# Attention and a four-expert mixture on one core: three preparations moved in the start of the program, and nine products put behind the last products with v

## The chip, the cores and the metric

The kernel runs on 1 core of one Trainium2 chip. The metric is device time in microseconds of one execution, the median of 3 runs. The matrix engine is called PE, its weight loads PEld; DVE, ACT, POOL and SP are the vector, scalar, GpSimd and sync engines. SP does no arithmetic here: it issues most of the DMAs.

## The reference

```python
def _attn_ref(q, k, v, n_global, n_local):            # (4, 8, 768, 64)
    scores = scale * np.matmul(q, k.transpose(0, 1, 3, 2))
    keep = is_global | is_local                        # 8 first keys, or 96 keys back
    scores = np.where(keep, scores + bias, -1e9)       # bias falls with distance, by head
    a = softmax(scores)
    return np.matmul(a, v)
def _moe_ref(x, domain_probs, w1, w2):                 # x: 3072 x 512, 4 experts, 1024 hidden
    p = domain_probs / (domain_probs.sum(-1, keepdims=True) + 1e-09)
    for e in range(E):
        h = np.maximum(x @ w1[e], 0.0)
        out += p[:, e:e + 1] * (h @ w2[e])
```

x is the attention's output, heads side by side. `domain_probs` is 3072 x 4 float32.

## The kernel before

**The work.** The rows are 4 batches of 768. The attention of batch 0 (`first_attention`) comes first and alone. The experts' products of batch 0 come next; beside them runs the attention of batches 1 to 3 (`attention`), and then the experts' products of batches 1 to 3 (`turned_batch`). A unit is one expert and 256 of its 1024 hidden columns, so a batch has 16 units. `first(i)` is x·w1 of unit i, `second(i)` is h·w2. The order is first(0), first(1), second(0), first(2), second(1) and so on.

**Products.** Each float32 operand is split in two rounded parts, high and low, and a product is three matmuls on them. x·w1 goes by a seven-product scheme of block matrices: on the weights' side A11, A12, A22 and the sums S1 to S4, on x's side B11, B21, B22 and the sums T1 to T4. `product(i, a, x)` is one of the seven, six matmuls of 384 columns into a PSUM tile `pm`, of which there are four in turn. The x side stands in tiles xB... and xT... that `forms_of` and `last_forms` fill: the high part by ACT (CAST), the low part by POOL or DVE (TENSOR_TENSOR). `load_w1` loads 512 KB of w1 into `raw`, POOL makes the four sums, and high and low parts go to `w1s`. `load_w2` does the same into `w2s`. A tile `raw` exists once for w1 and once for w2, so a load waits until the unit before is split. What has been split is written back to DRAM (`kept`) for the later batches.

**ReLU.** `relu` lets ACT write the high part of h, and `work_late` lets DVE write the low part later. A pm is free for another product only when both have read it.

**first_attention.** Twelve steps d work on two tiles of 128 rows for two heads each, in the order of pairs 0, 2, 1, 3. A step issues `scores` (PE), `softmax` (DVE: add bias and take the maximum, ACT: exponential), `turn` (PE transposes, DVE copies to pT), `turn_qk` (PE transposes of q and k of two steps later, ACT copies), `weigh_two` (PE: products with v and with the reciprocals; ACT copies the latter to rT) and `finish` (DVE multiplies into x). `weigh_two` has one PSUM tile, so that of step d can start only when `finish` of d - 1 has read it.

**Beside it.** The loop under `Ordered.on = True` hangs other work on the steps: `chores` are generators (`load_w1`, `load_w2`) that go on by one `yield` per step. Their arguments count steps: `load_w1(i, wait, lead, hold)` waits before the load, between load and sums, and between sums and split; `load_w2(i, lead, highs, gap)` waits `lead` steps between load and split and `gap` more between the two halves of the split. `mixture()` loads `prob`, and after its `yield` divides each row by its sum on DVE. After d = 13 comes the loop over `events`, which runs `first` and `second`. There instructions of DVE, ACT, POOL and SP keep the order of the program for the first `ONSTEPS` = 7 steps; after that a scheduler may place them.

**In steps 9 to 13** the loop starts `mixture()` (d = 9), starts `load_w2(0, ...)` (d = 10), and at d = 12 issues A11·B11 of unit 0 and the first half of A12·B21 (nine matmuls), ends the mixture and makes the form B21. At d = 13 it issues S1·T1 of unit 0 and A11·B11 of unit 1, and `last_forms`. Each of these comes after that step's own instructions, so what stands at d = 12 comes ahead of `weigh_two` of the last step, which belongs to d = 13.

Of the kernel before, what the change touches and what calls it, by code (L numbers as in the profile page):

```python
# [25 lines left out]
def f32(ap):  # L26
    return ap.bitcast(F32)
# [159 lines left out]
def attn_moe_kernel(ctx: ExitStack, tc, q, k, v, n_global, n_local, domain_probs, w1, w2, out):  # L187
# [19 lines left out]
    ve, ac, po, sy, te = (Ordered(tc, e) for e in (nc.vector, nc.scalar, nc.gpsimd, nc.sync, nc.tensor))  # L207
# [69 lines left out]
    def mixture():  # L277

        sy.dma_start(prob, domain_probs.rearrange("(t p) e -> p t e", p=P))
        yield  # L280

        psumm = fast.tile([P, P, 1], F32, name="psumm")[:, :NT]
        ve.reduce_sum(psumm, prob, axis=AX.X)
        ve.tensor_scalar_add(psumm, psumm, 1e-9)
        ve.reciprocal(psumm, psumm)
        ve.tensor_mul(prob, prob, psumm.to_broadcast([P, NT, E]))
# [213 lines left out]
    def first_attention(A, bank):  # L500
# [9 lines left out]
        def both(src, pr):  # L510
            return [src[0, 2 * pr + j].rearrange("(t p) d -> p t d", p=P) for j in range(2)]

        def start(pr, ts):
            if pr not in nats:
                nats[pr] = {m: A.nat.tile([P, NQT, 2, D], F32, name=f"first_{m}") for m in ("q", "k")}
            for m, src in (("q", q), ("k", k)):
                for j, rows in enumerate(both(src, pr)):
                    sy.dma_start(nats[pr][m][:, ts, j, :], rows[:, ts])

        def start_v(pr):  # L520
            vt, vg = (A.natv.tile([P, 2, NQT, D], F32, name=f"first_{m}") for m in ("v", "vg"))
            load_v(vt, vg, 0, pr)
            nats[pr]["v"], nats[pr]["vg"] = vt, vg
# [45 lines left out]
        def softmax(new):  # L569
            t, i, pr = new["t"], new["i"], new["pr"]  # L570
            bcol = slice(2 * P, 3 * P) if t == 0 else slice(0, 2 * P)
            pcol = slice(P, 2 * P) if t == 0 else slice(0, 2 * P)
            nmax = A.small.tile([P, 2], F32, name="nmax")
            new["pb"] = A.pb.tile([P, 2, 2 * P], F32, name="pb")
            for j in range(2):
                e = new["pb"][:, j, pcol]
                ve.tensor_tensor_reduce(
                    e, new["ps"][j], bias["n"][:, 2 * pr + j, bcol], 1.0, 3.0e38, ALU.add, ALU.min, nmax[:, j : j + 1]
                )
                ac.activation(e, e, AF.Exp, bias=nmax[:, j : j + 1], scale=-1.0, accum_out=new["z"][:, i, j : j + 1])  # L580
# [24 lines left out]
        def finish(d):  # L605
            pr, ts = tiles_of(d)
            ve.tensor_mul(x[:, pr, ts[0] * P : (ts[1] + 1) * P], pxs[d][:, : 2 * P], rTs[d])
# [9 lines left out]
        turn_qk(0)  # L617
        scores(0)
        start_v(ORDER[0])
        start(ORDER[1], slice(0, NQT))  # L620
        turn_qk(1)
        softmax(steps[0])
# [6 lines left out]
        for d in range(1, last + 3):  # L629
            if d + 1 <= last:  # L630
                scores(d + 1)
            if last - 1 <= d <= last + 1:
                finish(d - 3)
            if d <= last:
                softmax(steps[2 * d])
                softmax(steps[2 * d + 1])
            if d <= 3:
                next(spread)
            if 3 <= d < last - 1:
                finish(d - 3)  # L640
            if 1 <= d <= last + 1:
                for n in range(2):
                    turn(bank, A, steps[2 * d - 2 + n], ve.tensor_copy)
                recip(d - 1)
            if d + 2 <= last:
                turn_qk(d + 2)
            if d >= 2:
                weigh_two(d - 2)
            if d > last:
                finish(d - 2)  # L650
            if d % 3 == 1 and d // 3 + 2 < NPAIR:
                start(ORDER[d // 3 + 2], slice(0, NQT))
            if d % 3 == 2 and d // 3 + 2 < NPAIR:
                start_v(ORDER[d // 3 + 2])
            yield
# [157 lines left out]
    def load_w2(i, lead=7, highs=(ac.copy, ac.copy), gap=0):  # L813

        if i >= len(units):
            return
        b, e, g = units[i]
        if b >= TURNED and (e, g // 2) != (E - 1, NPR // 2 - 1):
            return
        if b > 0:  # L820
            wts[(i, 2)] = fetch("w2s", (e, g, 2), [P, 2, 2, DM], lambda t: t)
            return
        raw = rp.tile([P, 2, DM], F32, name="raw2")
        sy.dma_start(raw, w2[e, g * 2 * P : (g + 1) * 2 * P, :].rearrange("(a p) m -> p a m", p=P))
        for _ in range(lead):
            yield 1
        dst = wp.tile([P, 2, 2, DM], F32R, name="w2s")
        wts[(i, 2)] = dst
        for f in range(2):
            highs[f](dst[:, 0, f], raw[:, f])  # L830
            po.tensor_tensor(dst[:, 1, f], raw[:, f], f32(dst[:, 0, f]), op=ALU.subtract)
            yield 1
            for _ in range(gap * (1 - f)):
                yield 1
        waiting[(i, 2)] = (e, g, 2), dst
# [420 lines left out]
    chores = []  # L1256
# [17 lines left out]
    with ExitStack() as start_stack:  # L1274
        A = Pools(
            start_stack, "start",
            dict(setup=1, kd=2, qd=2, nat=2, natv=3, pb=6, pT=4, rT=2, small=6, sums=2), {},
        )
        for d, _ in enumerate(first_attention(A, bank)):
            if d == 0:  # L1280
                chores.append(load_w1(0, 0, 1, 1, po.tensor_copy))
            if d == 6:
                chores.append(load_w1(1, 0, 1, 0, po.tensor_copy))
            if d == 10:
                chores.append(load_w2(0, 2, (po.tensor_copy, ac.copy), 2))
            if d == 9:
                mix = mixture()
                next(mix)
            if d == 5:
                forms_of(0, ("B11", "T1"), ac.copy, po, ve, A)  # L1290
            if d == 8:
                forms_of(0, ("B21", "B22", "T3"), ac.copy, po, ve, A)
            if d == 9:
                forms_of(0, ("T2", "T4"), ac.copy, po, ve, A)
            if d == 11:
                forms_of(1, ("B11", "T1"), ac.copy, po, ve, A)
            if d == 12:
                p1, vv = up1.tile([P, HALF], F32, name="p1"), up.tile([P, HALF], F32, name="vv")
                ac.copy(p1, product(0, "A11", "B11")[:, :HALF])
                begun[1] = product(0, "A12", "B21", (0,))  # L1300
                next(mix, None)
                forms_of(1, ("B21",), ac.copy, ve, ve, A)
            if d == 13:
                begun[0] = p1, vv
                begun[2] = up1.tile([P, HALF], F32, name="p1")
                pms = product(0, "S1", "T1"), product(1, "A11", "B11")

                def take():
                    ve.tensor_add(vv, pms[0][:, :HALF], p1)
                    ac.copy(begun[2], pms[1][:, :HALF])  # L1310

                last_forms(1, take, A)
            work_chores()
    hp = early.enter_context(tc.tile_pool(name="hp", bufs=2))
    op = early.enter_context(tc.tile_pool(name="op", bufs=1))
    A = Pools(early, "att", dict(natv=1, ks=1, qs=1, nat=1, pb=2, pT=6, xt=2, small=2), {})
# [19 lines left out]
    for b in range(TURNED):  # L1336
        events = [(first, b * per)]
        for i in range(b * per + 1, (b + 1) * per):
            events += [(first, i), (second, i - 1)]
        events.append((second, (b + 1) * per - 1))  # L1340
        for n, (fn, i) in enumerate(events):
            if n == len(events) - 2:
                if b == TURNED - 1:
                    for _ in att:
                        pass
                chores.append(blocks(b + 1))
            if b == 0 and n == 0:
                chores += [load_w1(2, 1, 4, 1), load_w2(1, 6)]
            else:
                chores.append(load_w1(i + 2, 4) if fn is first else load_w2(i + 2))  # L1350
            if b == TURNED - 1 and n == len(events) - 12:
                chores.append(spread_shares())
            for _ in fn(i):
                work_chores()
                done += 1
                if done == ONSTEPS:
                    next(att)
                    check_sizes()
                    Ordered.on = False
                while emitted < count and emitted * (span - ONSTEPS) < (done - ONSTEPS) * count:  # L1360
                    next(att, None)
                    emitted += 1
# [43 lines left out]
```

## Time and profile before

| | |
|---|---|
| median of 3 runs | 1152.97 us (1152.83 to 1153.66) |
| the profiled execution: its time | 1152.95 us |
| its span, first to last instruction | 1151.2 us |
| PE busy | 1133.3 us (98%) |
| DVE busy | 890.4 us (77%) |
| POOL busy | 617.9 us (54%) |
| ACT busy | 551.7 us (48%) |
| mean granted TensorE clock | 0.999 of 2.4 GHz |

Times in rows are from the span's start; 1.75 us of the execution lie outside the span. A busy PE is one with a matmul in its pipeline, which does not say that it runs at its best rate. An idle engine is worth something only where PE in the end waits for it: PE is the engine with the least idle time, 17.9 us of the span.

### The profile page before, as it was taken

Reading aid. Unit: us, or ns where it says so; the run is one execution under the profiler, and the core shown is the slowest. Engines: PE = TensorE matmul, PEld = TensorE weight load, DVE = VectorE, ACT = ScalarE, POOL = GpSimd, SP = SyncE. Lnnn points to the kernel's source line nnn. Section 1 sums busy time; section 2 is a strip of 40 time slices with the busy share of each in tenths; the row PEclk is TensorE's granted clock in tenths of the full one; section 3 lists DMA queues with packets and bytes.
Section 4 is the critical chain, followed back from the end, with each engine's and each line's share of the span. In section 5 each row is a group of like instructions: output and inputs, shape, how many; then the busy total and the mean of one; then the engine's idle time right before and its main releaser. Section 6 shows DMA issues by size and latency. Waiting matters only on the chain.

```text
span 1151.2 us, 19555 instructions
## 1 busy us (share of the span) xinstructions
PE 1133.3 (98%) x7209; PEld 1064.8 (92%) x7209; DVE 890.4 (77%) x1618; ACT 551.7 (48%) x1337; POOL 617.9 (54%) x548
## 2 busy tenths in 40 slices
PE   8999999999999999999999999999999999999998
PEld 6778888888888889999999999999999899999996
DVE  6976677666676679788888867888889678888884
ACT  6748888788888733422222424222224253222231
POOL 5756434534343155766666357666662377766620
PEclk9999999999999999999999999999999999999999
DMA  8568887667876676666666565666666556666632
GB/s 204 138 201 312 266 258 225 222 211 220 272 252 218 209 277 231 227 222 229 243 243 241 195 211 214 227 222 224 262 239 235 213 202 234 219 233 220 219 120 95
DMA packets 184679, 256.26 MB, mean 223 GB/s; under 512 B 109216, under 2 KB 158976, under 8 KB 173568
## 3 DMA queue, kind: packets, MB, share of 16 engines
q1 hardware_dynamic: 177520, 231.34, 59.4%
q0 software_dynamic: 6048, 22.02, 5.0%
q10 hardware_dynamic: 1008, 1.57, 0.4%
q8 instruction: 59, 0.97, 0.3%
q14 instruction: 44, 0.36, 0.1%
HBM read 199.28 MB, written 55.62 MB: 221 GB/s over the span
## 4 chain that ended last, share of the span: by engine, by line
PE 83%; DVE 9%; ACT 4%; DMA 2%; issue 1%; SPq 1%; POOL 1%; ACTq 0%; DVEq 0%
PE pm L42 49%; PE pq L42 24%; PE pt L42 6%; PE ps L42 5%; DVE sumT L42 2%; DVE form L42 2%; DVE hB L42 1%; ACT pb L42 1%; DVE hT L42 1%; DMA w1s<-kept 1%; DVE pm L42 1%; DVE x L42 1%; DVE sumB L42 1%; SPq L42 1%; ACT form L42 0%
## 5 line engine op out<-in xcount | busy, mean ns | idle before, releaser
L42 PE MATMUL pm<-xT,w1s 128*128 128x384 f32 x1536 | 305.9, 336 | 0.8 <-DVE h L42 0.5
L42 PEld LDWEIGHTS pm<-xT,w1s 128*128 128x128 f32 x1536 | 268.3, 188 | 2.8 <-DVE h L42 1.6
L42 PE MATMUL pm<-xB,w1s 128*128 128x384 f32 x1152 | 224.7, 336 | 1.9 <-DVE hB L42 0.9
L42 PEld LDWEIGHTS pm<-xB,w1s 128*128 128x128 f32 x1152 | 201.0, 188 | 5.7 <-DVE hB L42 3.4
L42 POOL TENSOR_TENSOR raw<-raw 128x512 f32<-128x512 f32 x84 | 119.0, 1416 | 152.8 <-DMA raw<-in_moe_w_dram 147.8
L42 PE MATMUL pq<-form,w2s 128*128 128x384 f32 x1008 | 188.7, 334 | 0.0
L42 PEld LDWEIGHTS pq<-form,w2s 128*128 128x128 f32 x1008 | 176.0, 188 | 0.0
L42 PE MATMUL pm<-w2s,h 128*128 128x512 f32 x576 | 140.3, 395 | 1.6 <-DVE h L42 1.6
L42 PE MATMUL pq<-form,w2f 128*128 128x384 f32 x756 | 141.2, 334 | 0.0
L42 PEld LDWEIGHTS pq<-form,w2f 128*128 128x128 f32 x756 | 132.0, 188 | 0.0
L42 ACT CAST form<-hB 128x768 fp32r<-128x768 f32 x105 | 85.4, 836 | 92.4 <-DVE hB L42 92.4
L42 PEld LDWEIGHTS pm<-w2s,h 128*128 128x128 f32 x576 | 106.3, 188 | 22.9 <-POOL sums L42 1.5
L42 POOL TENSOR_TENSOR w2s<-raw,w2s 128x512 fp32r<-128x512 f32 x53 | 74.0, 1401 | 90.2 <-ACT w2s L42 78.4
L42 POOL TENSOR_TENSOR form<-hB,form 128x768 fp32r<-128x768 f32 x42 | 85.9, 2046 | 33.7 <-ACT form L42 33.7
L42 DVE TENSOR_TENSOR form<-hB,form 128x768 fp32r<-128x768 f32 x63 | 89.7, 1451 | 17.1 <-ACT form L42 16.8
L42 ACT ACTIVATE pb<-pb,nmax 128x256 f32<-128x256 f32 (+1 forms) x192 | 92.7, 488 | 11.4 <-DVE nmax L42 11.3
L42 ACT COPY p<-pm 128x384 f32<-128x384 f32 x64 | 30.7, 479 | 117.6 <-PE pm L42 117.4
L42 DVE SCALAR_TENSOR_TENSOR acc<-pm,prob,acc 128x512 f32<-128x512 f32 x90 | 67.0, 748 | 24.0 <-PE pm L42 23.1
L42 POOL TENSOR_TENSOR w2f<-raw,w2f 128x512 fp32r<-128x512 f32 x63 | 81.7, 1297 | 5.0
L42 POOL TENSOR_TENSOR w1s<-raw,w1s 128x512 fp32r<-128x512 f32 (+1 forms) x32 | 32.5, 1023 | 93.7 <-ACT w1s L42 93.3
L42 DVE TENSOR_TENSOR sumT<-pq,sumT 128x768 f32<-128x768 f32 x72 | 68.4, 950 | 17.4 <-PE pq L42 17.3
L42 DVE SCALAR_TENSOR_TENSOR hB<-pm,share 128x384 f32<-128x384 f32 x132 | 72.3, 553 | 6.7 <-PE pm L42 2.8
(157 smaller groups left out, 1795.6 us busy)
## 6 DMA issues: line engine op xcount, KB each, us to landing
w1s<-kept SPq DMA_DIRECT2D x48, 1792.0 KB, 8.6
w2s<-kept SPq DMA_DIRECT2D x126, 256.0 KB, 5.2
kept<-w1s SPq DMA_DIRECT2D x16, 1792.0 KB, 8.3
raw<-in_moe_w_dram POOLq DMA_DIRECT2D x42, 512.0 KB, 8.0
raw<-in_moe_w_dram SPq DMA_DIRECT2D x32, 512.0 KB, 4.5
kept<-w2s SPq DMA_DIRECT2D x16, 1024.0 KB, 7.1
w2s<-kept SPq DMA_DIRECT2D x6, 1024.0 KB, 4.8
v<-in_v_dram SPq DMA_DIRECT2D x12, 384.0 KB, 4.8
```

The lines of the kernel that those rows point to most:

```text
L42: ins = fn(*args, **kwargs)
```

## The change

Four edits, all in the start of the program.

1. The load of `prob` goes from step 9 to the start of first_attention, behind the loads of v of the first pair and ahead of those of q and k of the second pair. The four DVE instructions that normalize it go from d = 12 to d = 1.
2. `load_w2(0, ...)` has no gap: the second half of the split of unit 0's w2 comes two steps sooner.
3. The nine matmuls of A11·B11 and A12·B21, and the ACT copy that reads them, go from d = 12 to d = 13: behind weigh_two of the last step. The form B21 stays at d = 12.
4. `load_w1(2, ...)` waits for no step before its load, so that all of unit 2's w1 moves up by one step.

```diff
@@ first_attention @@
         start_v(ORDER[0])
+        mix = mixture()
+        next(mix)
         start(ORDER[1], slice(0, NQT))
...
                 softmax(steps[2 * d + 1])
+            if d == 1:
+                next(mix, None)
             if d <= 3:
@@ the loop around it @@
             if d == 10:
-                chores.append(load_w2(0, 2, (po.tensor_copy, ac.copy), 2))
-            if d == 9:
-                mix = mixture()
-                next(mix)
+                chores.append(load_w2(0, 2, (po.tensor_copy, ac.copy), 0))
...
             if d == 12:
+                forms_of(1, ("B21",), ac.copy, ve, ve, A)
+            if d == 13:
                 p1, vv = up1.tile([P, HALF], F32, name="p1"), up.tile([P, HALF], F32, name="vv")
                 ac.copy(p1, product(0, "A11", "B11")[:, :HALF])
                 begun[1] = product(0, "A12", "B21", (0,))
-                next(mix, None)
-                forms_of(1, ("B21",), ac.copy, ve, ve, A)
-            if d == 13:
                 begun[0] = p1, vv
@@ the loop over events @@
             if b == 0 and n == 0:
-                chores += [load_w1(2, 1, 4, 1), load_w2(1, 6)]
+                chores += [load_w1(2, 0, 4, 1), load_w2(1, 6)]
```

On SP, in the first microseconds: first_q and first_k are loads for batch 0, raw_248 and raw_249 are unit 0's w1. Before:

```order
L42 DMA first_v<-in_v_dram 128x12x64
L42 DMA first_vg<-in_v_dram 96x12x64
L42 DMA first_vg<-in_v_dram 32x6x64 x2
L42 DMA first_q<-in_q_dram 128x6x64 x2
L42 DMA first_k<-in_k_dram 128x6x64 x2
L42 DMA raw_248<-in_moe_w_dram 128x4x256
```

Now:

```order
L42 DMA first_v<-in_v_dram 128x12x64
L42 DMA first_vg<-in_v_dram 96x12x64
L42 DMA first_vg<-in_v_dram 32x6x64 x2
L42 DMA prob<-in_moe_domain_probs_dram 128x24x4
L42 DMA first_q<-in_q_dram 128x6x64 x2
L42 DMA first_k<-in_k_dram 128x6x64 x2
L42 DMA raw_249<-in_moe_w_dram 128x4x256
```

The load of prob, 128 x 24 pieces of 4 numbers, stands ahead of q and k of the second pair.

On PE, at the end of batch 0's attention: ps<-pT,... are products with v, ps<-ident,zr the reciprocals, pm<-xB... and pm<-xT... products with w1.

```order
 L42 MATMUL ps<-pT,first_v 64x128 x2
 L42 MATMUL ps<-ident,zr 64x128 x4
-L42 MATMUL pm<-xB_577,w1s 128x384 x6
-L42 MATMUL pm<-xB_775,w1s 128x384 x3
 L42 MATMUL ps<-pT,first_vg 64x128 x2
 L42 MATMUL ps<-pT,first_v 64x128 x2
```

The nine products no longer stand between the last two groups of products with v; they follow the second.

On ACT, where first(0) begins: h<-pm is a ReLU, p a copy of a product; raw_913 and raw_918 are unit 0's w2, raw_1121 and raw_1125 unit 1's w2, raw_1132 and raw_1123 unit 2's w1. Before:

```order
L42 COPY p_1038<-pm 128x384
L42 ACTIVATE h<-pm 128x384
L42 CAST w2s<-raw_913 128x512
L42 ACTIVATE h<-pm 128x384 x2
L42 CAST w2s<-raw_1121 128x512
L42 ACTIVATE h<-pm 128x384
L42 CAST w1s<-raw_1132 128x512
L42 CAST w2s<-raw_1121 128x512
```

Now:

```order
L42 COPY p_1038<-pm 128x384
L42 CAST w2s<-raw_918 128x512
L42 ACTIVATE h<-pm 128x384
L42 CAST w1s<-sums 128x512
L42 CAST w2s<-raw_1125 128x512
L42 ACTIVATE h<-pm 128x384
L42 CAST w1s<-sums 128x512
L42 ACTIVATE h<-pm 128x384 x2
L42 CAST w1s<-raw_1123 128x512
```

The cast of unit 1's w2 stood behind the third of unit 0's four ReLUs; it now stands behind the first, with a cast of unit 2's sums ahead of it.

## Rows read from the trace of the kernel before

**Rows 1.** Busy time by stretch: us, then busy (count) by engine, clock, DMA share, GB/s.

```profile
core 0: us, PE busy (x) PEld busy (x) DVE busy (x) ACT busy (x) POOL busy (x), PEclk, DMA share, GB/s
12.00:17.00 5.00, 3.66 (x28) 2.51 (x29) 2.93 (x14) 4.03 (x17) 0.00 (x1) 1.00 1.04 259
17.00:47.00 30.00, 29.99 (x336) 24.55 (x335) 27.17 (x99) 25.54 (x100) 24.52 (x29) 1.00 0.88 219
...
61.50:78.00 16.50, 13.74 (x71) 11.84 (x71) 12.89 (x27) 8.25 (x17) 5.78 (x7) 1.00 0.70 222
78.00:450.00 372.00, 371.44 (x2658) 328.47 (x2659) 259.50 (x707) 277.92 (x818) 161.78 (x162) 1.00 0.74 244
```

**Rows 2.** Timeline of PE: start, duration, what, count, idle time before and its releaser.

```profile
14.76 0.41 PE L42 MATMUL ps<-ident,first_k 128*128 128x128 f32 x2 [0.41 <-DMA first_k<-in_k_dram]
```

**Rows 3.** Timeline of SP: DMA issues.

```profile
10.28 1.13 SPq L42 DMA_DIRECT2D first_k<-in_k_dram  x2
...
32.60 0.39 SPq L42 DMA_DIRECT2D raw<-in_moe_w_dram  x1
33.03 0.51 SPq L42 DMA_DIRECT2D prob<-in_moe_domain_probs_dram  x1
33.58 2.95 SPq L42 DMA_DIRECT2D raw<-in_moe_w_dram  x1
...
68.46 0.90 SPq L42 DMA_DIRECT2D raw<-in_moe_w_dram  x2
```

**Rows 4.** Tile view of first_k, issues at 10.3 and 10.9 us: from issue to landing.

```profile
DMA to landing us min/median/max: 3.1/3.4/3.8
```

**Rows 5.** Tile view of prob: from issue to landing.

```profile
DMA to landing us min/median/max: 4.8/4.8/4.8
```

**Rows 6.** Tile view of raw, the issue at 32.60 us: from issue to landing.

```profile
DMA to landing us min/median/max: 3.8/3.8/3.8
```

**Rows 7.** Timeline of DVE, 12 to 74 us, seven of its rows.

```profile
13.74 1.13 DVE L42 COPY pT<-pt 128x256 f32<-128x256 f32 x2 [1.53 <-PE pt L42]
...
57.85 0.42 DVE L42 TENSOR_TENSOR x<-ps,rT 128x256 f32<-128x256 f32 x1 [0.33 <-ACT rT L42]
...
59.62 0.26 DVE L42 TENSOR_TENSOR prob<-prob,psumm 128x96 f32<-128x96 f32 x1
...
61.09 0.42 DVE L42 TENSOR_TENSOR x<-ps,rT 128x256 f32<-128x256 f32 x1 [0.74 <-ACT rT L42]
...
67.07 0.55 DVE L42 TENSOR_TENSOR vv<-pm,vv 128x384 f32<-128x384 f32 x1
...
69.11 0.56 DVE L42 SCALAR_TENSOR_TENSOR h<-pm,h 128x384 fp32r<-128x384 f32 x1
...
73.78 0.56 DVE L42 SCALAR_TENSOR_TENSOR h<-pm,h 128x384 fp32r<-128x384 f32 x1 [2.06 <-ACT h L42]
```

**Rows 8.** Timeline of PE, 55 to 87 us, seven of its rows.

```profile
55.81 0.44 PE L42 MATMUL ps<-pT,first_vg 128*64 128x128 f32 x4 [0.35 <-DVE x L42]
...
57.27 1.85 PE L42 MATMUL pm<-xB,w1s 128*128 128x384 f32 x9
59.05 0.44 PE L42 MATMUL ps<-pT,first_vg 128*64 128x128 f32 x4
...
60.51 1.31 PE L42 MATMUL pm<-xT,w1s 128*128 128x384 f32 x6
...
64.62 2.36 PE L42 MATMUL pm<-xT,w1s 128*128 128x384 f32 x12 [0.19 <-ACT p L42]
67.21 3.84 PE L42 MATMUL pm<-xT,w1s 128*128 128x384 f32 x18 [0.23 <-DVE h L42]
...
78.00 8.46 PE L42 MATMUL pm<-w2s,h 128*128 128x512 f32 x36 [1.23 <-DVE h L42]
```

**Rows 9.** Timeline of ACT, 66 to 74 us, two of its rows.

```profile
66.46 0.61 ACT L42 CAST w2s<-raw 128x512 fp32r<-128x512 f32 x1
...
72.73 0.62 ACT L42 CAST w2s<-raw 128x512 fp32r<-128x512 f32 x1 [2.07 <-DMA raw<-in_moe_w_dram]
```

**Rows 10.** Timeline of POOL, one row.

```profile
67.15 1.29 POOL L42 TENSOR_TENSOR w2s<-raw,w2s 128x512 fp32r<-128x512 f32 x1 [7.93 <-ACT w2s L42]
```

## The prediction

> **What bounds the kernel now.** I read the busy times by stretch first. From 78 to 450 us PE is busy 371.44 of 372 us [rows 1]. Whatever moves its first matmul there, the product h·w2 of unit 0 at 78.00 [rows 8], moves the end by as much; what is prepared sooner for later units buys nothing, because PE waits for none of it. So the question is when PE reaches that matmul. Before it there are three places where it waits. Around 14 us it stands 0.41 us for the keys of the second pair [rows 2]; from 17 to 47 us it is busy 29.99 of 30 us, so a delay at 14 us is carried through [rows 1]. Around 50 to 58 us, at the end of batch 0's attention, a group of products with v waits for DVE to empty the one PSUM tile [rows 8]. From 61.5 to 78 us PE is idle 2.76 us [rows 1], mostly because a ReLU's low part on DVE comes late and a `pm` is not free. The DVE timeline gives that its cause: at 73.78 DVE has stood 2.06 us for ACT [rows 7], and ACT stood 2.07 us in a cast that waited for unit 1's w2 from DRAM [rows 9]. That load was issued at 68.46 [rows 3], when POOL's second half of unit 0's w2 (67.15, 1.29 us) let go of `raw` [rows 10, 3].
>
> **The change, part by part.** The time is made against the profiled execution, 1152.95 us (its span is 1151.2); the median of the runs shown is 0.02 us above it.
>
> *The load of prob, sooner.* It is placed ahead of q and k of the second pair, whose last load is issued at 10.9 and lands 3.8 us later, at 14.7 [rows 4]; PE starts on it at 14.76 [rows 2]. There is no slack, and nothing can come out of this but a delay. The lower end is the issue alone: prob at 33.03, the next at 33.58 [rows 3], 0.55 us. The middle is its transfer: it landed at 33.03 + 4.8 = 37.8, the load issued ahead of it at 32.60 + 3.8 = 36.4 [rows 3, 5, 6], so it held the DMA engines 1.4 us. The upper end is the issue after it, which took 2.95 us where the like one took 0.39 [rows 3]: SP stood 2.5 us behind prob. The DMA engines are full where the load now goes (share 1.04 from 12 to 17 us, [rows 1]), so I take most of the transfer: **+1.2 us**, ends 0.55 and 2.5. The loads of batch 0 behind it in SP's queue are late by as much, and so is PE that wants them. POOL's queue is passed by nothing.
>
> The Trainium skill (DMA: Bandwidth & Descriptors, section Bandwidth, its table of measured sizes) gives a floor of about 10.5 ns a packet for small transfers. The 3,072 pieces of prob would take 32 us by it one after another, which the landing after 4.8 us denies [rows 5]; shared by 16 engines they would take 2.0 us, an estimate from that page, and with it in place of 1.2 the sum would be 1155.45.
>
> *The mixture's four DVE instructions.* They now stand ahead of the first copies to pT, before which DVE is idle 1.53 us from 12.2 on [rows 7]. In the old place they took 59.88 - 58.27 = 1.6 us [rows 7]. Prob lands by 9.2 + 4.8 = 14.0 at the latest by the old figure, so DVE could be done at 15.6, 1.9 us late; 1.2 us of that is PE's own delay, and DVE has 2.8 us of idle time from 17 to 47 us to catch up [rows 1]. Cost 0, upper end +0.7. Taking them out at 58 us is worth nothing by itself: the next row that matters, the last piece of x at 61.09, waited 0.74 us for ACT and not for them [rows 7]. They would be in the way after the next edit.
>
> *The nine products behind the last products with v.* Before, these products of 1.78 us (57.27 to 59.05, [rows 8]) lay over the wait for DVE's read at 57.85 to 58.27 [rows 7]. Now PE stands until 58.3 and starts the last products with v there instead of at 59.05. From that start to the last piece of x it is 61.09 - 59.05 = 2.04 us, so x is there at 60.3: **-0.74 us** for DVE's chain of forms. PE, though, gets to S1·T1 at 58.3 + 1.46 + 1.78 = 61.55 and not at 60.51 [rows 8]: **+1.05 us** for PE. Which of the two decides? DVE's sum of vv and S2·T2 at 67.07 [rows 7] begins as the twelve products from 64.62 end, at 66.98 [rows 8]: PE decides. With the 0.19 us wait gone that sum starts at about 67.9, +0.8.
>
> *Unit 0's w2 sooner, and unit 1's.* The cast is now ahead of the first ReLU: it can start when the copy of A11·B11 of unit 1 is made: twelve matmuls behind 61.55, and the copy, about 64.4. POOL's half follows and ends at 66.4, unit 1's w2 is issued then, 2 us sooner, and as before lands 4.25 us later (68.46 to 72.73, [rows 3, 9]), at 70.7. That looks like 2 us gained on the wait at 72.73. But the order on ACT has changed: that cast now stands ahead of the second ReLU of unit 0, where it stood ahead of the fourth. The second ReLU's input is ready at 67.9 + 0.9 + 0.6 = 69.4; ACT gets to it after the cast's 0.6 us [rows 9], at 71.3. Its low part on DVE starts at 71.7 instead of 69.11 [rows 7]. Behind it in DVE's queue wait the remaining sums of unit 0, and on PE the product S1·T1 of unit 1, which needs that `pm`: 72.3. Five more products of six matmuls at 197 ns (2.36 us for 12, [rows 8]) take 5.9 us, and I leave 0.3 us for the next low part: PE is at h·w2 at 78.5, where it was at 78.00. Together with the edit before: **+0.5 us**. The lower end, should ACT not hold the ReLU: 75 matmuls from 61.55 on without a wait make 76.35, -1.65. The upper end, should DVE fall behind a second time by as much as the 0.7 that its chain already lags: +1.2.
>
> *Unit 2's w1 sooner.* Its load goes ahead of batch 1's v in SP's queue and lands before 60 us. POOL's sums follow the split of w2. PE first wants the result at 87 us and does not wait there today [rows 1]. Worth 0; its casts on ACT are part of the jam above.
>
> **Sum:** 1152.95 + 1.2 + 0.5 = 1154.65, against the median 1154.7.
>
> **The rivals.**
> *A, the preparations pay:* prob costs its issue alone, and the cast of unit 1's w2 finds its data, so that no ReLU is held. Then PE runs from S1·T1 to h·w2 unbroken: 1152.95 + 0.55 - 1.65 = 1151.85. For it: the load does go out 2 us sooner, and the wait that it removes is the longest on that path. Against it: the order on ACT, and 4.25 us from issue to landing. It decides for A if the load lands before 69.4, which needs an issue at 65.1.
> *B, SP is held behind prob:* if SP stands 2.5 us there as it did at 33.58, the keys land near 17.1 and the sum is 1152.95 + 2.5 + 0.5 = 1155.95, slower. For it: that one row [rows 3]. Against it: there a load of the w1 kind was still under way, and the keys' loads already queue in the full rings today, part of which time the hold would replace. It decides from a hold of about 1.8 us on.
> *C, prob's many small pieces hold more than the bytes say:* prob took 4.8 us to land, the keys' load with four times its bytes 3.1 at best [rows 4, 5]. If these 1.7 us come on top of the issue's 0.55, the delay is 2.25 and the sum 1155.7, slower. Against it: that landing had a load of 512 KB just ahead [rows 3, 6]. It decides from about 1.8 us on. By the page's rate above, shared by 16 engines, it would be 1155.45.
> *D, the edits cancel:* prob fills gaps in the DMA engines and costs 0.55 to 0.8, the rest as forecast: 1153.9 to 1154.3, no change that can be told. I count it with the forecast.
>
> **How the numbers follow.** 0.2% is 2.3 us, about what a measurement of this kernel can tell from no change: faster means under 1150.7, slower over 1155.3. Forecast with D 0.52, A 0.18, B 0.2, C 0.1. A alone stays inside 0.2%; only with 1.2 us more, from nothing that I can name, would it come below: 0.04. B is slower nearly always (0.17), C in two cases of three (0.07), the forecast at its upper end (0.05): 0.29. No change: 0.67. The range is from A's figure, 1151.8, to B's with the upper part of its own spread, 1156.5; what lies beyond has about 0.15. The forecast's own range is 1153.6 to 1155.5.
>
> **What would show it.** In the profile of the changed kernel the first transposes of the second pair's keys should start at 15.6 to 16.2 and wait over 1 us for their DMA; the row of SP behind prob tells B from the forecast. DVE's normalization should end before 15.7 and no PE wait should name it. The last piece of x should stand 0.3 to 0.6 us later than 61.09, the two effects together. ACT should show an idle time of 1 us or more in front of a cast of w2s between the first and second ReLU of unit 0, and PE one wait of about 1 to 2.5 us for h near 73, where there were several short ones; h·w2 should start near 79.7. From there on the two traces should run at one distance. The prediction is wrong if the keys wait no longer than today, if the second ReLU follows the first within 3 us, or if a new wait appears after 80 us, which I have priced at nothing.

## The result and the profile after

The changed kernel takes 1161.54 us (1160.54 to 1161.87, 4 runs), the kernel before 1153.32 us (1152.83 to 1155.09, 4 runs) beside it: 8.2 us slower, ratio 1.0065, 95% interval 1.0053 to 1.0077. The prediction was 1154.7 us in a range from 1151.8 to 1156.5; the time lies 5.0 us above the upper end.

| | before | after |
|---|---|---|
| the profiled execution | 1152.95 us | 1161.87 us |
| its span | 1151.2 us | 1159.8 us |
| PE busy | 1133.3 us (98%) | 1137.3 us (98%) |
| DVE, ACT, POOL busy | 890.4, 551.7, 617.9 us | 889.1, 551.6, 618.0 us |
| mean granted TensorE clock | 0.999 | 0.995 |

PE's busy time rose by 4.0 us although it does the same products, and its idle time by 4.6 us (22.5 of 1159.8 us where it was 17.9). The windows of the changed kernel show where the busy time grew: busy time by stretch, with the granted clock as the third number from the end, 1.00 for 2.4 GHz and 0.50 for 1.2 GHz.

```profile
12.00:17.00 5.00, 2.35 (x16) 1.53 (x16) 4.11 (x20) 2.64 (x11) 0.31 (x1) 1.00 0.98 195
17.70:24.50 6.80, 5.89 (x30) 4.54 (x32) 2.29 (x9) 3.65 (x14) 4.92 (x6) 0.50 1.02 237
...
72.00:79.00 7.00, 4.42 (x24) 3.78 (x23) 3.81 (x8) 2.63 (x6) 5.87 (x7) 1.00 0.89 298
79.20:82.50 3.30, 3.14 (x11) 2.86 (x10) 2.31 (x6) 1.59 (x4) 2.87 (x4) 0.50 1.13 283
```

There are two stretches at half clock. Each follows one in which PE had little to do: 2.35 of 5 us, and 4.42 of 7 us. In rows 1 the clock was 1.00 throughout.

**The first place.** SP's timeline, first before, then after (start, duration, what it issued):

```profile
9.20 1.03 SPq L42 DMA_DIRECT2D first_q<-in_q_dram  x2
```

```profile
9.73 0.44 SPq L42 DMA_DIRECT2D prob<-in_moe_domain_probs_dram  x1
10.22 2.48 SPq L42 DMA_DIRECT2D first_q<-in_q_dram  x2
12.74 1.61 SPq L42 DMA_DIRECT2D first_k<-in_k_dram  x2
```

PE's timeline at that place, before and after (idle time before an entry and its releaser in brackets):

```profile
15.91 0.98 PE L42 MATMUL pm<-early_k,early_q 64*128 64x128 f32 x8 [0.74 <-ACT early_k L42]
16.82 1.09 PE L42 MATMUL pt<-ident,pb 128*128 128x128 f32 x8
...
19.52 1.13 PE L42 MATMUL pm<-early_k,early_q 64*128 64x256 f32 x8
```

```profile
15.61 0.41 PE L42 MATMUL ps<-ident,first_q 128*128 128x128 f32 x2 [1.11 <-DMA first_q<-in_q_dram]
17.88 0.66 PE L42 MATMUL ps<-ident,first_k 128*128 128x128 f32 x2 [1.85 <-DMA first_k<-in_k_dram]
19.27 1.66 PE L42 MATMUL pm<-early_k,early_q 64*128 64x128 f32 x8 [0.74 <-ACT early_k L42]
20.86 1.97 PE L42 MATMUL pt<-ident,pb 128*128 128x128 f32 x8
...
25.28 1.13 PE L42 MATMUL pm<-early_k,early_q 64*128 64x256 f32 x8
```

SP stands 1.45 us longer in the issue of q, PE waits for q (new) and for k (1.85 where it was 0.41, [rows 2]), and k's transposes start at 17.88 and not at 14.76: 3.12 us late. Of this 0.53 us stood already when SP came to prob (9.73, where q went out at 9.20 before), ahead of anything that the change touches. Such differences are scatter of single executions: where the start of the program is as before, k's transposes begin anywhere from 14.76 (before) and 14.81 (before_held, below) to 15.70 (no_mix_held). Then the same eight score matmuls take 1.66 us and not 0.98, the same eight transposes 1.97 and not 1.09. At 25.28, the next scores, PE is 5.76 us late: 2.64 us more were lost while it worked, without a wait for a load.

**The second place.** The end of attention and first(0), after: ACT, DVE and PE.

```profile
71.28 0.49 ACT L42 ACTIVATE h<-pm 128x384 fp32r<-128x384 f32 x1 [0.78 <-issue]
74.23 0.62 ACT L42 CAST w1s<-sums 128x512 fp32r<-128x512 f32 x1 [2.46 <-PE pm L42]
76.40 0.62 ACT L42 CAST w2s<-raw 128x512 fp32r<-128x512 f32 x1 [1.55 <-DMA raw<-in_moe_w_dram]
76.92 0.48 ACT L42 ACTIVATE h<-pm 128x384 fp32r<-128x384 f32 x1
```

```profile
66.11 0.42 DVE L42 TENSOR_TENSOR x<-ps,rT 128x256 f32<-128x256 f32 x1 [0.75 <-ACT rT L42]
...
77.44 0.56 DVE L42 SCALAR_TENSOR_TENSOR h<-pm,h 128x384 fp32r<-128x384 f32 x1 [2.35 <-ACT h L42]
```

```profile
78.05 1.43 PE L42 MATMUL pm<-xT,w1s 128*128 128x384 f32 x6 [2.52 <-DVE h L42]
79.64 2.29 PE L42 MATMUL pm<-xT,w1s 128*128 128x384 f32 x6 [0.16 <-DVE h L42]
81.73 2.63 PE L42 MATMUL pm<-xB,w1s 128*128 128x384 f32 x12
84.20 1.20 PE L42 MATMUL pm<-xT,w1s 128*128 128x384 f32 x6
85.24 8.37 PE L42 MATMUL pm<-w2s,h 128*128 128x512 f32 x36
...
97.39 0.97 PE L42 MATMUL ps<-ks,qs 64*128 64x256 f32 x12 [0.88 <-DVE ks L42]
```

The second ReLU stands on ACT behind a cast that waits for unit 1's w2 (76.40), its low part on DVE comes at 77.44, and PE waits 2.52 us for it in one piece, where before it had several shorter ones, the longest 1.23 us [rows 8]. Then PE runs at half clock again: six matmuls take 2.29 us where they took 1.31 [rows 8].

Further on PE has a wait that it did not have. Batch 1's first scores, before:

```profile
89.47 0.98 PE L42 MATMUL ps<-ks,qs 64*128 64x256 f32 x12
```

The distances add up. Keys +3.12 and half clock +2.64 make +5.76 at 25.28. The last piece of x is 0.74 us less late than that: 66.11 against 61.09, [rows 7], is +5.02. h·w2 of unit 0 stands at 85.24 against 78.00, +7.24. Batch 1's first scores stand at 97.39 against 89.47, 0.68 more, with the wait of 0.88 us for ks in front. Another 0.7 us are lost in small pieces to the span's end, and 0.3 us outside it: 8.9 us between the two profiled executions.

### The profile page after: what moved, and what is told of

The parts are those of the page before. It is cut to its first block, busy times and chain, and to the rows that moved or that the text cites. A ratio compares the mean times of both kernels' runs of the same rounds, so it can differ in the third digit from the quotient of the medians.

```text
span 1159.8 us, 19553 instructions
## 1 busy us (share of the span) xinstructions
PE 1137.3 (98%) x7209; PEld 1068.5 (92%) x7209; DVE 889.1 (77%) x1618; ACT 551.6 (48%) x1337; POOL 618.0 (53%) x548
## 4 chain that ended last, share of the span: by engine, by line
PE 82%; DVE 9%; ACT 3%; DMA 3%; issue 1%; SPq 1%; POOL 0%; DVEq 0%; ACTq 0%
PE pm L42 49%; PE pq L42 23%; PE pt L42 6%; PE ps L42 5%; DVE sumT L42 2%; DVE hB L42 2%; DVE form L42 1%; DMA w1s<-kept 1%; ACT pb L42 1%; SPq L42 1%; DVE sumB L42 1%; DVE x L42 1%; DVE pm L42 1%; DVE hT L42 1%; DMA w2s<-kept 0%
```

## The experiments

A theory was set up from these traces. **T**: the load of prob holds SP and the DMA engines, PE idles, and idling is followed by half clock; near 75 us the same happens because ACT stands in casts with a ReLU queued behind. The medians below stand beside that of the kernel before, measured side by side with it. The ratios, with their 95% intervals, lie a little under the quotients of the medians. Mean granted clocks are listed for every execution, stretches only for the profiled one.

### Each part alone

only_mix is the kernel before with edit 1:

```diff
         start_v(ORDER[0])
+        mix = mixture()
+        next(mix)
...
+            if d == 1:
+                next(mix, None)
...
-            if d == 9:
-                mix = mixture()
-                next(mix)
...
-                next(mix, None)
```

> Before with the mixture's edit alone. Theory T: of the 8.2 us, the start makes 5.4 to 6.1: SP stands 2.5 us behind prob's load, q and k of the second pair land 3 us late, and PE's idle time of 3 us there is followed by a stretch of some 7 us at half the granted clock. So 1158.7 to 1159.4 us, keys at 17.5 to 18, granted clock under 0.7 from 17 to 25 us and 1.00 from 61 to 90 us. Rival R1, the half clock belongs to no edit: keys as late, no half clock or one elsewhere, 1156.3. Rival R2, everything comes from the start, and the trouble near 75 us is only its echo: 1161.5.

Measured: 1159.12 us beside 1153.76, ratio 1.0038 (1.0025 to 1.0051). SP's issue of q, and PE:

```profile
9.75 2.81 SPq L42 DMA_DIRECT2D first_q<-in_q_dram  x2
```

```profile
16.92 0.66 PE L42 MATMUL ps<-ident,first_k 128*128 128x128 f32 x2 [0.99 <-DMA first_k<-in_k_dram]
...
24.19 1.13 PE L42 MATMUL pm<-early_k,early_q 64*128 64x256 f32 x8
```

As T has it in kind: SP is held 1.78 us, keys are 2.16 us late, and at 24.19 PE is 4.67 us late; the clock is 0.50 from 16.5 to 23.2 us. Both the hold and the delay are less than T had (2.5 us, keys at 17.5 to 18). This edit alone makes more than half of the loss.

only_nine is the kernel before with edit 3 (the nine products moved from d = 12 to d = 13):

```diff
             if d == 12:
-                p1, vv = up1.tile([P, HALF], F32, name="p1"), up.tile([P, HALF], F32, name="vv")
-                ac.copy(p1, product(0, "A11", "B11")[:, :HALF])
-                begun[1] = product(0, "A12", "B21", (0,))
...
             if d == 13:
+                p1, vv = up1.tile([P, HALF], F32, name="p1"), up.tile([P, HALF], F32, name="vv")
+                ac.copy(p1, product(0, "A11", "B11")[:, :HALF])
+                begun[1] = product(0, "A12", "B21", (0,))
```

> Before with the nine products moved alone. Theory T: the last piece of x comes 0.7 us sooner and nothing is lost by it; the loss near 75 us belongs to the casts of ACT that edits 2 and 4 put ahead of the second ReLU. So 1152.6 to 1153.6. Rival R3, the loss near 75 us belongs to this edit, because PE's products for x come later while ACT's cast still waits for unit 1's w2: PE idle over 2 us before h·w2, 1155 to 1156. Rival R2: no change, 1153.3.

Measured: 1156.88 us beside 1153.76, ratio 1.0026 (1.0018 to 1.0035). Theory T missed here; rival R3 was near, 0.9 us below. ACT, then PE:

```profile
69.10 0.49 ACT L42 ACTIVATE h<-pm 128x384 fp32r<-128x384 f32 x1 [2.39 <-DVE pm L42]
72.70 0.62 ACT L42 CAST w2s<-raw 128x512 fp32r<-128x512 f32 x1 [3.11 <-DMA raw<-in_moe_w_dram]
73.22 0.86 ACT L42 ACTIVATE h<-pm 128x384 fp32r<-128x384 f32 x2
```

```profile
74.35 2.29 PE L42 MATMUL pm<-xT,w1s 128*128 128x384 f32 x6 [2.77 <-DVE h L42]
```

R3 named the wait of PE and the cast, but not what changed on ACT. The new order of the program has also moved the cast of unit 1's w2 on ACT: it stood behind the third of unit 0's ReLUs and now stands behind the second, so that ACT stands 3.11 us for a load with two ReLUs behind it. PE idles 2.77 us, and from 73.1 to 79.8 us the clock is 0.50. So this edit alone makes a trap of the same kind as edits 2 and 4.

only_w is the kernel before with edits 2 and 4:

```diff
-                chores.append(load_w2(0, 2, (po.tensor_copy, ac.copy), 2))
+                chores.append(load_w2(0, 2, (po.tensor_copy, ac.copy), 0))
...
-                chores += [load_w1(2, 1, 4, 1), load_w2(1, 6)]
+                chores += [load_w1(2, 0, 4, 1), load_w2(1, 6)]
```

> Before with edits 2 and 4 alone (w2 of unit 0 without its gap, w1 of unit 2 a step sooner). Theory T: the casts ahead of the second ReLU cost what they cost in the changed kernel, some 2.2 us, with an idle time of PE over 2 us near 72 us and the half clock behind it: 1155 to 1156. Rival R3: 1152.8 to 1153.5, no such wait. Rival R2: 1153.3.

Measured: 1155.41 us beside 1153.76, ratio 1.0009 (1.0001 to 1.0018): the smallest part, and the one that differs most from execution to execution, from 1152.88 us (mean clock 0.999) to 1157.67 (0.995). T's time is met by the median; its wait of over 2 us is not there. PE waits 0.69 and 1.26 us for h near 75 us.

no_mix is the changed kernel with edit 1 taken back (prob loaded at d = 9 and normalized at d = 12, as before):

```diff
-        mix = mixture()
-        next(mix)
         start(ORDER[1], slice(0, NQT))
...
+            if d == 9:
+                mix = mixture()
+                next(mix)
...
```

> The changed kernel with the mixture put back where it was. Theory T: keys at 14.8 us, granted clock 1.00 from 17 to 25 us, and what is left is the loss near 75 us with a PE wait over 2 us for h and half the clock behind it: 1155.1 to 1156.0. Rival R1: a stretch at half clock in the first 30 us all the same, 1158. Rival R2: 1153.3, no loss at 75 us without the late start.

Measured: 1158.0 us beside 1153.76, ratio 1.0028 (1.0018 to 1.0038): 4.2 us by the medians, over T's range. Rival R2 falls: the loss near 75 us does not need the late start. PE waits 2.17 us for h (to 74.23), and half clock follows. But what R1 forecast for this run came too: 1158 us and half clock in the first 30 us. In the profiled execution, as in only_w's, the clock is 0.50 from 10.1 to 16.8 us, where the program is as before (see the last section). The first scores of the second pair are 2.27 us late by it (18.18 against 15.91), which is most of the 3.23 us by which h·w2 is late (81.23 against 78.00). So 4.2 us is too much for edits 2 to 4. The executions fall in two groups: four with a mean clock of 0.997 or 0.998 took 1155.77 to 1156.94 us, five with 0.994 to 0.996 took 1158.00 to 1159.59. If the early half clock is what parts them (one of the five was traced), these edits cost some 2 to 3 us, an estimate from the first four.

### What in the load costs

mix_act is only_mix with the load on ACT's queue; mix_whole is only_mix with prob in 128 pieces of 384 bytes and not 3,072 of 16. In mix_whole the shares then go to other rows, so it is there for its time alone:

```diff
-        sy.dma_start(prob, domain_probs.rearrange("(t p) e -> p t e", p=P))
+        ac.dma_start(prob, domain_probs.rearrange("(t p) e -> p t e", p=P))
```

```diff
-        sy.dma_start(prob, domain_probs.rearrange("(t p) e -> p t e", p=P))
+        sy.dma_start(prob, domain_probs.rearrange("(p t) e -> p t e", p=P))
```

> only_mix with prob's load issued by ACT and not by SP. Theory S, what costs is that SP stands behind prob's issue: SP issues q and k at 9.2 and 10.3 as before, the transposes of k start by 15.6, total 1153.3 to 1155.0. Rival P, what costs is the transfer of prob's 3,072 pieces on the DMA engines, whoever issues them: q and k are issued on time, yet land late, transposes of k at 16.5 or later, total 1156 to 1159.

> only_mix with prob loaded in 128 pieces of 384 bytes in place of 3,072 of 16. Each partition then holds 24 rows that follow each other, so the mixture's shares go to other rows: timing only. Theory S and P both make it cheap if the number of pieces is the cause: SP's next issue takes about 1.1 us, transposes of k by 15.5, 1153.5 to 1155. Rival W, any transfer put in there costs as much, because the rings are full: SP's next issue takes over 2 us as in only_mix, 1157.5 to 1159.5.

Measured beside 1153.92: mix_act 1154.38 us, ratio 1.0005 (0.9996 to 1.0014); mix_whole 1154.28 us, ratio 1.0005 (0.9997 to 1.0014). Neither can be told from no change. Of mix_act the queue that carried prob (packets, MB, share of 16 engines from 5 to 20 us), and PE at the keys:

```profile
q10 hardware_dynamic: 3088, 0.05, 11.6%
```

```profile
15.53 0.41 PE L42 MATMUL ps<-ident,first_k 128*128 128x128 f32 x2 [0.81 <-DMA first_k<-in_k_dram]
```

Of mix_whole SP's issue of q, and PE at the keys:

```profile
9.73 1.02 SPq L42 DMA_DIRECT2D first_q<-in_q_dram  x2
```

```profile
15.38 0.41 PE L42 MATMUL ps<-ident,first_k 128*128 128x128 f32 x2 [1.11 <-DMA first_k<-in_k_dram]
```

In 128 pieces the same 48 KB hold SP no longer than their own issue: q goes out at 9.73 and not at 9.20, and q's issue takes 1.02 us. The keys are 0.62 us later than before, within the scatter above. Rival W falls: the number of pieces is the cause, not the place as such. In mix_act the 3,072 pieces still take 11.6% of 15 us, 1.74 us of each DMA engine, but they went out 2.4 us sooner, at 6.9, on a queue of their own, and SP issued q in 1.06 us. SP's issue of k then took 2.21 us where it was 1.13 [rows 3], and the keys are 0.77 us later than before, so some of the hold may still be there. The time speaks for theory S against P; as the load was also earlier, this run does not show the two apart by itself.

### Does idling bring the half clock?

mix_fill puts idle products in front of the late transposes of only_mix:

```diff
             for n, m in enumerate(("q", "k")):
+                for _ in range((5, 4)[n] if d == 3 else 0):
+                    te.matmul(tp[:, n * 2 * P : n * 2 * P + P], ident, ident, start=True, stop=True)
```

> only_mix with nine idle products of the unit matrix on PE in front of the late transposes: five ahead of those of q, four ahead of those of k, into PSUM that the transposes then overwrite. Nothing waits less for it. Theory T, the half clock follows PE's idle time: the transposes of k start at 16.9 as before or at most 0.3 us later, the granted clock from 17 to 25 us is 1.00, the scores of the second tile pair come 2.0 to 2.8 us sooner than in only_mix, total 1156.2 to 1157.2. Rival R1, the clock falls for another reason (the phase of the execution, the DMA load): a half clock stretch as in only_mix, 1159 to 1159.5.

Measured: 1158.13 us beside 1153.92, ratio 1.0041 (1.0029 to 1.0053), above T's range. The profiled execution, 1155.78 us, is as T has it: clock 1.00, keys at 16.72, and the next scores, in PE's timeline,

```profile
21.47 1.14 PE L42 MATMUL pm<-early_k,early_q 64*128 64x256 f32 x8
```

2.7 us sooner than in only_mix. The other executions lay between 1156.12 and 1160.46 us with mean clocks down to 0.996, and no trace shows where they lost it. By its median this run settles nothing, and only its trace speaks for T.

So the cost was measured by itself, in the kernel before with its loads untouched. idle3 lets ACT make PE wait; idle3_fill gives PE idle products in that gap:

```diff
             qT, kT = gots[pr]["q"], gots[pr]["k"]
+            if d == 3:
+                idle = A.setup.tile([P, 2 * P], F32, name="idle")
+                for _ in range(10):
+                    ac.copy(idle, nats[pr]["q"].rearrange("p t j d -> p (t j d)")[:, : 2 * P])
```

```diff
             got, at = gots[pr], 0
+            for _ in range(14 if d == 3 else 0):
+                te.matmul(pss[0][:, :P], ident, ident, start=True, stop=True)
```

> The kernel before, its loads untouched, with ten idle copies on ACT ahead of the copies of the second pair's first q and k, so that PE stands some 3.5 us in one piece between 15.2 and 18.7 us, for ACT and for no DMA. Theory T, the half clock follows PE's idle time: scores of that step 2 to 3 us late by the wait, then a stretch at half clock, and by 25 us PE is 4 to 5.5 us late; total 1157.3 to 1159.2. Rival R1, the half clock of the other runs belongs to the late DMA or to chance: clock 1.00, PE is 2 to 3 us late and stays so, 1155.3 to 1156.8.

> idle3 with fourteen idle products of the unit matrix on PE in that gap; they wait for nothing and are overwritten. Theory T: the scores as late as in idle3, but no half clock; 1155.3 to 1157.0, and under idle3 by 1.5 to 2.8 us. Rival R1: as idle3, within 0.7 us of it.

Measured beside 1153.39: idle3 1157.48 us, ratio 1.0035 (1.0021 to 1.0049); idle3_fill 1155.69 us, ratio 1.0023 (1.0014 to 1.0033). PE's timeline of idle3 and a window of it:

```profile
15.63 0.41 PE L42 MATMUL ps<-ident,first_k 128*128 128x128 f32 x2 [1.40 <-DMA first_k<-in_k_dram]
18.96 1.66 PE L42 MATMUL pm<-early_k,early_q 64*128 64x128 f32 x8 [2.92 <-ACT early_k L42]
20.55 1.97 PE L42 MATMUL pt<-ident,pb 128*128 128x128 f32 x8
...
24.13 1.13 PE L42 MATMUL pm<-early_k,early_q 64*128 64x256 f32 x8
```

```profile
19.00:22.40 3.40, 3.40 (x17) 2.75 (x18) 0.69 (x1) 2.16 (x9) 3.32 (x4) 0.50 1.01 228
```

The same of idle3_fill:

```profile
14.43 0.41 PE L42 MATMUL ps<-ident,first_k 128*128 128x128 f32 x2 [0.20 <-DMA first_k<-in_k_dram]
14.67 3.29 PE L42 MATMUL pm<-ident 128*128 128x128 f32 x28
18.96 0.98 PE L42 MATMUL pm<-early_k,early_q 64*128 64x128 f32 x8 [0.99 <-ACT early_k L42]
...
22.57 1.13 PE L42 MATMUL pm<-early_k,early_q 64*128 64x256 f32 x8
```

```profile
19.00:22.40 3.40, 3.40 (x40) 2.90 (x40) 1.80 (x7) 2.95 (x12) 3.29 (x4) 1.00 0.90 204
```

Both kernels start the scores at 18.96. The one in which PE stood idle goes on at half clock and is at the next scores at 24.13; the other, in which PE did useless work instead, goes on at full clock and is there at 22.57. The medians differ by 1.79 us, the traces by 1.56. One thing more differs in the two traces: idle3's keys landed 1.20 us later, by scatter, so PE had stood 1.40 us there before its 2.92 us. Two things speak against this late load as the cause. In no_mix_held (below) the keys were as late, at 15.70 with a wait of 1.43 us, and without the second wait the clock stayed at 1.00. And the clocks differ in nearly all executions: all five of idle3 have a mean of 0.998 or less, nine of ten of idle3_fill 0.999 or more. So PE's idle time brings the half clock here, and R1 falls for this pair.

### ACT's order

no_mix_held keeps the casts of unit 2's w1 and unit 1's w2 in the order of the program on ACT, which puts them behind unit 0's four ReLUs; before_held does that to the kernel before:

```diff
+            held = lambda *a: tc.keep_in_program_order(nc.scalar.copy(*a))
             if b == 0 and n == 0:
-                chores += [load_w1(2, 0, 4, 1), load_w2(1, 6)]
+                chores += [load_w1(2, 0, 4, 1, held), load_w2(1, 6, (held, held))]
```

> no_mix with the casts of unit 2's w1 and of unit 1's w2 kept in the order of the program on ACT, which puts them behind unit 0's four ReLUs. Theory A, the second loss is ACT standing in a cast with ReLUs queued behind it: no wait of PE for h over 1 us, h·w2 at 76 to 77.5, no half clock near 75 to 82 us; a later wait can take some of it back; 1152 to 1154.5. Rival N, the loss comes from the later place of the nine products on PE and DVE whatever ACT does: PE still waits 2 us for h, 1156.5 to 1158.5.

> The kernel before with nothing but the casts of unit 2's w1 and unit 1's w2 kept in program order on ACT, behind unit 0's ReLUs. Theory A: the 2.06 us of DVE for ACT near 73.8 and PE's wait of 1.23 us before h·w2 go, h·w2 at 76.5 to 77.2 in place of 78.0, and if nothing comes up later 1152.0 to 1153.3. Rival N: ACT's order is worth nothing, 1153.5 to 1154.5, or the casts come late and a product with unit 2's w1 waits, over 1154.5.

Measured: no_mix_held 1152.63 us beside 1153.92, ratio 0.9993 (0.9985 to 1.0002); before_held 1153.33 us beside 1153.39, ratio 0.9998 (0.9989 to 1.0007). no_mix_held, ACT and PE:

```profile
71.44 0.96 ACT L42 ACTIVATE h<-pm 128x384 fp32r<-128x384 f32 x2 [1.10 <-DVE pm L42]
72.29 0.92 ACT L1347 CAST w1s<-raw 128x512 fp32r<-128x512 f32 x2
73.11 0.62 ACT L1347 CAST w2s<-raw 128x512 fp32r<-128x512 f32 x1
```

```profile
72.58 1.31 PE L42 MATMUL pm<-xT,w1s 128*128 128x384 f32 x6 [0.27 <-DVE h L42]
...
76.85 8.37 PE L42 MATMUL pm<-w2s,h 128*128 128x512 f32 x36
...
89.13 0.97 PE L42 MATMUL ps<-ks,qs 64*128 64x256 f32 x12 [1.01 <-DVE ks L42]
```

Theory A holds. With edits 2, 3 and 4 in place and only the casts held back, PE's wait of 2.17 us is gone and the clock stays at 1.00 in that trace; h·w2 starts at 76.85, 1.15 us sooner than in the kernel before [rows 8], although PE waited 1.4 us for the keys where it was 0.41 [rows 2]. The medians of no_mix and no_mix_held, which did not run side by side, lie 5.4 us apart, of which no_mix's early half clock is a part; but even the fastest execution of no_mix, 1155.77 us, is slower than ten of the eleven of no_mix_held. In before_held h·w2 comes at 76.87 too, as forecast, but the time lies at the very end of theory A's range, 1152.0 to 1153.3: a wait of 1.05 us for POOL's sums is the next to end last, and the median is that of the kernel before.

held_turn is no_mix_held with a step more ahead of batch 1's first scores:

```diff
         turn_qk(bank, nats[jobs[0]], gots[jobs[0]], 0)
         yield
+        yield
```

> no_mix_held with one step more between the transposes of batch 1's first q and k and the scores that use them. In no_mix_held PE waits 1.01 us for DVE's ks there. Theory: that wait goes, 0.5 to 1 us under no_mix_held, 1151.6 to 1152.5, and against the kernel before faster by 0.1 to 0.2%. Rival: the step shifts the rest of the attention beside the experts, and the time is as no_mix_held's or above, 1152.6 to 1155.

Measured: 1152.76 us beside 1153.39, ratio 0.9991 (0.9982 to 1.0000). The wait for ks stays, 0.96 us: the rival is right. One of its eleven executions took 4057 us, was not traced and is left out of the comparison; I would not take this kernel. None of the three is faster than the kernel before by 0.2%. What removes the wait for ks, which the kernel before does not have, was not found.

## Why the prediction was wrong

Two terms of the sum failed, and one place that was priced at nothing. Prob's load was put at +1.2 us and cost about 2.6; the clock had no term and cost about 4; a new wait after 80 us took 0.7 more.

**Where the bound lies: right for a delay, not for a gain.** The late keys were carried through to h·w2: in only_mix the scores are 4.67 us late at 24.19, and h·w2 starts at 82.71, 4.71 us late. But "whatever moves its first matmul there moves the end by as much" did not hold the other way: in no_mix_held h·w2 is 1.15 us sooner and batch 1's first scores only 0.34 (89.13 against 89.47), because the wait for ks came up.

**"So I take most of the transfer: +1.2 us": too small.** The keys were late by some 2.6 us by the load in the changed kernel (3.12 less the 0.53 that SP was late already), and by 2.1 in only_mix (2.16 less 0.06). This is the size of rivals B and C, which had 2.5 and 2.25, and both their mechanisms were there: SP's longer stand in q's issue, and 3,072 pieces that take 1.74 us of each DMA engine in all (mix_act). The argument against B, that the hold would replace time in which the keys' loads queue anyway, failed. The page's rate for small transfers in the Trainium skill (DMA: Bandwidth & Descriptors, section Bandwidth) gave an estimate of 2.0 us where I took 1.2 from two landings. The 1.74 us of mix_act's trace are nearer to that estimate; the page gives its rate for loads issued from GpSimd, and sharing it by 16 engines was my step, not the page's.

**The missing term: the clock.** "A delay at 14 us is carried through" took for granted that PE does the same work at the same rate behind a wait. No rival priced that the rate falls. It cost 2.64 us at the first place and some 1.3 at the second (2.09 us from start to start for the six matmuls from 79.64, 2.47 for the twelve from 81.73, against 1.15 and 2.08 in no_mix_held). These 4 us are nearly half of the loss. Even rival B's delay in the sum, 1155.95, stayed under 1156.5 us.

**The mixture's DVE instructions at nothing: right.** No wait of PE names them; PE's wait behind them is for q. It does not need this cover: in mix_act PE waits 0.81 us for the keys there, and for nothing of DVE either.

**"-0.74 us" for the last x: right to 0.01.** 61.09 + 5.76 would be 66.85; it came at 66.11. But only_nine shows that the edit is not worth taking alone, since it moves a cast on ACT as well.

**ACT's jam: right in its mechanism and its times.** I forecast the second ReLU's low part at 71.7 and S1·T1 of unit 1 at 72.3 for a start without delay; 77.44 and 78.05 less 5.76 are 71.68 and 72.29. h·w2, forecast at 78.5, came at 79.48 by that count, and 1.3 us of it are the clock: without it, it would have been 0.3 us early. That these times agree to 0.02 us is in part luck, as both are sums of several steps; that ACT would hold the second ReLU behind the cast was foreseen.

**"Which I have priced at nothing": a new wait after 80 us.** 0.88 us for ks, in no_mix_held 1.01. only_w has it with 0.88 us and only_nine not at all, so edits 2 and 4 bring it; but edit 1 alone brings 0.60 us of it too (only_mix, for ACT's part of ks), and mix_act and mix_whole 0.44 and 0.33. What sets it is open.

The parts do not add up exactly: 5.4 for edit 1 and 4.2 for the rest are 9.6 us, where the whole cost 8.2. no_mix's share holds the early half clock, 2.27 us in its trace, which the trace of the changed kernel does not have; how the executions that were not traced share it is not known.

## What to carry to other kernels

A wait of PE can cost more than its length: where a change can make PE stand as long as here (2.2 to 3 us), add what the work behind it costs at half the clock (1.3 to 2.6 us a time in these traces), as a term or as a rival. A load ahead of others that PE waits for is to be priced by its number of pieces too: here 48 KB cost nothing that could be told in 128 pieces, and 5.4 us (by the medians, with the clock) in 3,072. And look at what stands behind each instruction that waits for a load, as on ACT here, where the ReLUs came only after the cast: only_nine and no_mix both lost time to a cast of weights that PE did not need yet and that stood ahead of a ReLU.

## What the runs showed of the hardware

The granted clock is not the same in all executions of one program. In the profiled execution of only_w it was 0.50 from 10.2 to 16.9 us, where its work is that of the kernel before, in whose trace it was 1.00 there:

```profile
7.00:10.00 3.00, 1.69 (x14) 1.12 (x16) 1.81 (x12) 1.39 (x6) 0.23 (x1) 1.00 1.00 228
10.20:16.90 6.70, 5.96 (x27) 4.01 (x24) 2.90 (x14) 4.35 (x19) 2.03 (x2) 0.50 0.95 223
```

In front of it PE had only its short waits, 1.69 us busy of 3, and it brought the first scores of the second pair 2.3 us late (18.21 against 15.91). That low share does not decide it: the changed kernel has the same 1.68 us of 3 there and keeps the full clock.

```profile
7.00:10.00 3.00, 1.68 (x14) 1.11 (x16) 1.80 (x12) 1.38 (x6) 0.23 (x1) 1.00 1.03 235
```

Nor does it need one long wait: in only_w the clock is 0.50 again from 75.0 to 78.4 us, and ahead of it PE's longest wait was 1.26 us, with 1.34 us busy of 3 from 72 to 75. And a wait is not always followed by half clock: in no_mix_held PE waited 1.43 us for the keys and ran on at 1.00. What decides in each execution, no run here shows.
